# Running decay preparation, attention and gated MoE of three groups of tokens side by side, with squares on ACT, the cosine by Abs and the state's scale carried by v

## The chip, the cores and the metric

The kernel runs on one core of a Trainium2 chip. The metric is device time in microseconds (us). Every kernel here was run several times, always beside runs of the kernel before on the same chip. The record marks a run as slow when it is over 1.5% above the fastest run of the same kernel; comparisons use the fast runs alone. ACT is the engine of activation functions, DVE the vector engine, POOL the GpSimd engine, PE the matmul engine, SP the queue that issues most transfers (SPq in the views), PEld the weight loads of PE. PSUM tiles hold the results of this kernel's matmuls. MoE is the gated layer after the attention. A slab is 128 tokens by 384 features (8 heads of 48); there are 24 slabs.

## The reference, cut to what matters

```python
# attention: q, k, v, a_re, a_im of shape (4, 8, 768, 48)
mag = np.sqrt(a_re * a_re + a_im * a_im)
scale = np.minimum(mag, 0.999) / (mag + 1e-06)
a = (a_re + 1j * a_im) * scale            # written here as one complex number
for t in range(S):
    state = a[:, :, t, :, None] * state + k_t (outer) v_t
    y[:, :, t] = q_t @ real(state)
# MoE: x = y as (3072, 384); w_gate, w_val (384, 1536); w_out (1536, 384)
out = (sigmoid(x @ w_gate) * (x @ w_val)) @ w_out
```

The kernel turns the recurrence into matmuls inside slabs: the logarithms of the magnitudes are summed along the tokens by a matmul with a triangular matrix (`cl`), so are the angles (`ct`), and q and k are multiplied by the exponentials, sines and cosines of the sums.

## The kernel before

Eight groups of three slabs each. In the first half of a period PE has the attention of group g, the output projection of g-1 and the decays of g+1 (`prep_a`); in the second half gate and value of g and the angles of g+1 (`prep_b`). ACT's instructions stay in the order in which the program gives them.

Names in the code and in the views: `cl` and `ct` are the summed logarithms and angles (the matmul with `nid_t` takes whole turns `r` off the angles), `cs` their cosine and sine, `kst` and `qst` the products of k and q with them. In attention `tp` are the transposes of q and k (`qkT` their copy), `sc` the scores (`mst` masked), `kv`, `u`, `P` and `x` belong to the state, `xp` are the transposes of y. In the MoE `pg`, `pv` and `po` are the matmuls of gate, value and output, `g` is the tanh of the gate, `p` gate times value. `lm`, new in the changed kernel, is the squared magnitude and then its logarithm.

```python
    def prep_a(g):                                   # decays
        nc.scalar.preload_act_table_set("natural_log_exp_and_others")      # L157
        nc.scalar.activation(out=ar, in_=ar, func=FT.Ln)
        nc.scalar.activation(out=inv, in_=ar, func=FT.Exp, scale=-1.0)
        yield
        for s in range(NS):
            G.last_pool = nc.gpsimd.tensor_tensor(                         # L162
                out=ai[:, s], in0=ai[:, s], in1=inv[:, s], op=ALU.mult)
            nc.scalar.activation(out=inv[:, s], in_=ai[:, s], func=FT.Square)
            nc.scalar.activation(out=inv[:, s], in_=inv[:, s], func=FT.Ln, bias=1.0)
            nc.vector.scalar_tensor_tensor(                                # L167
                out=ar[:, s], in0=ar[:, s], scalar=2.0, op0=ALU.mult,
                in1=inv[:, s], op1=ALU.add)
            nc.vector.tensor_scalar(out=ar[:, s], in0=ar[:, s],            # L170
                                    scalar1=LN_CAP, scalar2=None, op0=ALU.min)
            yield
        # ... per slab: cl = wl_t @ ar (L176), two Exp of cl, products with q and k on POOL
    # prep_b, cosine of one slab:
            r2 = psm.tile([L, HD], F16, name=f"r2_{g}_{s}", tag="r2")
            nc.vector.tensor_scalar(out=r2, in0=ct, scalar1=0.25,          # L229
                                    scalar2=None, op0=ALU.is_gt)
            nc.tensor.matmul(ct, nid_t, r2, start=False, stop=True, ...)
            nc.scalar.activation(out=cs[:, 0], in_=ct, func=FT.Sin,
                                 scale=TWO_PI, bias=pio2)
    # attn, one slab: state (u, x16, kv), transposes, scores, y, transposes of y;
    # then the next slab.  main loop:
        for g in range(NG):
            st = [(attn(g), 21)]
            if g > 0:
                st.append((outproj(g - 1), 9))
            if g + 1 < NG:
                loads_a(g + 1); loads_q(g + 1)
                st.append((prep_a(g + 1), 7))
            merge(*st)
            st = [(gateval(g), 12)]
            if g + 1 < NG:
                st.append((prep_b(g + 1), 4))
            merge(*st)
```

## Time and profile before

| | before |
|---|---|
| time, median of 3 runs | 383.69 us |
| span of the profiled run | 382.3 us |
| ACT's log table loads for the decays of groups 1 to 7 | 46.29 to 302.22 us, so 42.7 us a period |
| from the last of these loads to the end | 80.1 us |
| granted PE clock, mean | 0.902 |

One more view is needed for what came later, the groups of instructions on PE. In a row, after the bar come busy time and mean ns of one, then the idle time of PE just before these instructions and who ended it.

```profile
L176 PE MATMUL cl<-a,wl_t 128*128 128x384 f32 x48 | 29.8, 724 | 14.3 <-DVE a L170 14.3
L296 PE MATMUL sc<-qkT 128*128 128x128 f16 x192 | 21.9, 245 | 22.1 <-DVE qkT L288 21.9
L319 PE MATMUL xp<-idn_t,y 128*128 128x128 f16 x72 | 9.5, 250 | 14.9 <-ACT y L314 14.6
```

PE stood 37 us in all in front of the scores (sc) and the transposes of y (xp), which depend on a result made moments before, and 14 us in front of the decay matmul cl. The 14 us all lie in the start, before 46.29 us.

### The profile page before, as it was taken

The page shows a single profiled execution, that of the slowest core. Times are in us where ns is not written, and L with a number is a line of the kernel's source. Part 1 is how long each engine was busy: PE and PEld are TensorE (multiplying, and loading weights), DVE is VectorE, ACT ScalarE, POOL GpSimd, SP SyncE. Part 2 cuts the span into 40 slices and gives each one's busy share as a digit, 9 for nine tenths or more (in the row PEclk, how much of TensorE's full clock was granted, in tenths as well). Part 3 has the DMA queues.
Part 4 walks back from the last instruction along what each step waited for, and adds up shares of the span by engine and source line. Part 5 has one row for each costly group of instructions (what it writes and reads, how often), then busy time and mean ns, then how long its engine had stood idle before and what let it go on. Part 6 is the DMA issues. An engine that isn't in the chain of part 4 may idle for free.

```text
span 382.3 us, 6035 instructions
## 1 busy us (share of the span) xinstructions
PE 291.6 (76%) x2208; PEld 179.5 (47%) x2208; DVE 244.3 (64%) x451; ACT 199.8 (52%) x343; POOL 107.1 (28%) x114
## 2 busy tenths in 40 slices
PE   0451448899579958898679958898679958998796
PEld 0121135456445636455445536465445645555463
DVE  1325476478735994678736895688727995589450
ACT  2650253846467554846376554747375645731241
POOL 0755444412353035302152035303132035200000
PEclk9988557999799987999699988999699988999899
DMA  9998993996654771465432772054410002000101
GB/s 155 191 204 127 197 172 63 141 176 119 127 97 77 119 144 43 63 100 87 103 70 37 105 144 44 1 107 83 103 22 3 0 22 42 2 0 22 43 2 62
DMA packets 150989, 32.68 MB, mean 85 GB/s; under 512 B 145048, under 2 KB 150192, under 8 KB 150960
## 3 DMA queue, kind: packets, MB, share of 16 engines
q1 hardware_dynamic: 148368, 28.76, 42.5%
q0 software_dynamic: 2592, 3.54, 5.2%
q8 instruction: 17, 0.28, 0.3%
q14 instruction: 12, 0.10, 0.1%
HBM read 31.07 MB, written 4.76 MB: 94 GB/s over the span
## 4 chain that ended last, share of the span: by engine, by line
issue 33%; PE 26%; DVE 12%; ACT 9%; POOL 7%; DMA 6%; SPq 5%; POOLq 0%; ACTq 0%
PE cl L176 6%; DMA qk<-in_k_dram 5%; DVE mst L300 4%; PE pg L330 4%; DVE a L167 3%; PE po L347 3%; PE pv L334 3%; POOL run L217 3%; SPq L109 3%; DVE qkT L288 2%; ACT y L314 2%; POOL a L162 2%; PE xp L319 2%; PE tp L285 2%; PE tp L284 2%
## 5 line engine op out<-in xcount | busy, mean ns | idle before, releaser
L330 PE MATMUL pg<-xt,wg 128*128 128x384 f16 x288 | 64.5, 329 | 7.5 <-ACT g L337 5.7
L191 POOL TENSOR_TENSOR qk<-qk,ee 128x768 f32<-128x768 f32 x24 | 43.9, 1829 | 74.4 <-ACT ee L179 45.2
L334 PE MATMUL pv<-xt,wv 128*128 128x384 f16 x288 | 63.2, 329 | 0.0
L338 DVE SCALAR_TENSOR_TENSOR p<-g,pv 128x384 f16<-128x384 f16 x96 | 49.4, 549 | 21.1 <-ACT g L337 17.6
L162 POOL TENSOR_TENSOR a<-a,inv 128x384 f32<-128x384 f32 x24 | 24.8, 1060 | 114.3 <-ACT inv L159 114.3
L337 ACT ACTIVATE g<-pg 128x384 f16<-128x384 f32 x96 | 43.9, 489 | 21.7 <-PE pg L330 21.6
L347 PE MATMUL po<-wo,p 128*128 128x384 f16 x288 | 54.7, 325 | 0.1
L330 PEld LDWEIGHTS <-wg 128*128 128x128 f16 x288 | 28.3, 98 | 35.3 <-issue 18.5
L288 DVE COPY qkT<-tp 128x1024 f16<-128x1024 f16 x48 | 32.3, 684 | 13.9 <-PE tp L285 13.7
L176 PE MATMUL cl<-a,wl_t 128*128 128x384 f32 x48 | 29.8, 724 | 14.3 <-DVE a L170 14.3
L296 PE MATMUL sc<-qkT 128*128 128x128 f16 x192 | 21.9, 245 | 22.1 <-DVE qkT L288 21.9
L334 PEld LDWEIGHTS <-wv 128*128 128x128 f16 x288 | 28.4, 99 | 19.9 <-issue 1.6
L221 DVE TENSOR_SCALAR r<-ct 128x384 f16<-128x384 f32 x24 | 13.3, 554 | 33.3 <-PE ct L210 17.8
L233 ACT ACTIVATE cs<-ct,pio 128x384 f32<-128x384 f32 x24 | 14.0, 581 | 38.9 <-PE ct L231 38.9
L300 DVE TENSOR_TENSOR mst<-sc,msk_t 128x512 f16<-128x512 f32 x48 | 31.4, 681 | 3.3 <-PE sc L296 3.2
L347 PEld LDWEIGHTS <-p 128*128 128x128 f16 x288 | 25.9, 97 | 14.6 <-issue 1.1
L284 PE MATMUL tp<-idn_t,qst 128*128 128x128 f16 x192 | 32.7, 250 | 0.0
L285 PE MATMUL tp<-idn_t,kst 128*128 128x128 f16 x192 | 32.3, 250 | 0.0
L177 ACT ACTIVATE ee<-cl 128x384 f32<-128x384 f32 x24 | 11.8, 492 | 37.4 <-PE cl L176 37.4
L237 DVE TENSOR_TENSOR qst<-qk,cs 128x768 f16<-128x768 f32 x24 | 23.0, 958 | 12.3 <-ACT cs L233 10.6
L296 PEld LDWEIGHTS <-qkT 128*128 128x128 f16 x192 | 14.1, 108 | 35.6 <-DVE qkT L288 31.4
L314 ACT ACTIVATE y<-y 128x384 f16<-128x384 f32 x24 | 11.7, 489 | 36.5 <-PE y L311 36.5
(57 smaller groups left out, 498.4 us busy)
## 6 DMA issues: line engine op xcount, KB each, us to landing
a<-in_a_re_dram SPq DMA_DIRECT2D x24, 192.0 KB
a<-in_a_im_dram SPq DMA_DIRECT2D x24, 192.0 KB
qk<-in_q_dram SPq DMA_DIRECT2D x24, 192.0 KB
qk<-in_k_dram SPq DMA_DIRECT2D x24, 192.0 KB
v<-in_v_dram SPq DMA_DIRECT2D x24, 192.0 KB
out_dram<-ot SPq DMA_DIRECT2D x24, 192.0 KB
wg<-in_moe_w_gate_dram POOLq DMA_DIRECT2D x3, 384.0 KB, 9.0
wv<-in_moe_w_val_dram POOLq DMA_DIRECT2D x3, 384.0 KB, 8.7
```

Of the source, the lines that this page charges most:

```text
L176: nc.tensor.matmul(cl, wl_t, ar[:, s], start=True, stop=True)
L191: nc.gpsimd.tensor_tensor(out=G.qk[:, :, s], in0=G.qk[:, :, s], in1=G.ee[:, :, s], op=ALU.mult)
L284: nc.tensor.transpose(tp[:, i], qs[:, h], idn_t)
L285: nc.tensor.transpose(tp[:, 4 + i], ks[:, h], idn_t)
L288: nc.vector.tensor_copy(out=qkT, in_=tp)
L296: nc.tensor.matmul(sc[:, i], qkT[:, 4 + i], qkT[:, i], start=True, stop=True)
L300: nc.vector.tensor_tensor(out=mst, in0=sc, in1=msk_t.unsqueeze(1).broadcast_to([L, 4, L]), op=ALU.mult)
L330: nc.tensor.matmul(pg, wg16[:, j, fc], G.xt[:, j], start=(j == 0), stop=(j == 2))
L334: nc.tensor.matmul(pv, wv16[:, j, fc], G.xt[:, j], start=(j == 0), stop=(j == 2))
L337: nc.scalar.activation(out=g16, in_=pg, func=FT.Tanh, scale=0.5)
L338: nc.vector.scalar_tensor_tensor(out=G.p[:, fb], in0=g16, scalar=1.0, op0=ALU.add, in1=pv, op1=ALU.mult)
L347: nc.tensor.matmul(po, G.p[:, fb, s * L:(s + 1) * L], wo16[:, fb], start=(fb == 0), stop=(fb == NFB - 1))
```

## The change

Its intent: (1) three stages at once, attention of group i, MoE of i-1 and i-2, preparation of i+1, so that large MoE matmuls stand beside every short dependent one; groups of uneven size (1, 2, 3 x 6, 2, 1), so that the pipeline fills and drains on small groups; (2) the decays from |a| squared: squares on ACT, add and clamp on POOL, one Ln for a group, which frees DVE; (3) the cosine as sin(pi/2 - |x|), with Abs on ACT in place of a comparison on DVE and a second matmul; (4) the scale 1024 of the state carried by v, so that DVE does not multiply it in; (5) inside attention, the transposes of slab s stand ahead of the end of slab s-1. Cut to its core (buffers, tile shapes and names left out):

```diff
-    NS = 3
+    SIZES = [1, 2, 3, 3, 3, 3, 3, 3, 2, 1]
     def prep_a(g):
-        (Ln, Exp; per slab: POOL product, ACT Square, ACT Ln, DVE add, DVE min)
+        nc.scalar.activation(out=sq[:, :, :n], in_=G.a2[:, :, :n], func=FT.Square)   # L162
+        for s in range(n):
+            nc.gpsimd.tensor_tensor(out=G.lm[:, s], in0=sq[:, 0, s],                 # L165
+                                    in1=sq[:, 1, s], op=ALU.add)
+            nc.gpsimd.tensor_scalar(out=G.lm[:, s], in0=G.lm[:, s], scalar1=CAP,     # L167
+                                    scalar2=-1.0, op0=ALU.min, op1=ALU.max)
+        nc.scalar.activation(out=ar, in_=ar, func=FT.Ln)
+        nc.scalar.activation(out=ar, in_=ar, func=FT.Exp, scale=-1.0)
+        yield
+        nc.scalar.activation(out=lm, in_=lm, func=FT.Ln)                             # L173
     # prep_b
-            nc.vector.tensor_scalar(out=r2, in0=ct, scalar1=0.25, op0=ALU.is_gt, ...)
-            nc.tensor.matmul(ct, nid_t, r2, ...)
+            nc.scalar.activation(out=cs[:, 0], in_=ct, func=FT.Abs)
     # attn
-                nc.vector.tensor_scalar(out=x16, in0=u, scalar1=YSC, op0=ALU.mult)
+                nc.gpsimd.tensor_copy(out=X[s], in_=u)
-        for each slab: state, turn 0, turn 1, score 0, score 1, yout, xput
+        for s in range(n + 1):
+            turn(s, 0); turn(s, 1); state(s)       # if s < n
+            xput(s - 1)                            # if s > 0
+            score(s, 0); score(s, 1); yout(s)      # if s < n
     # main loop, iteration i
+            merge(first 2/5 of attn(i), outproj(i - 2), prep_a(i + 1))
+            merge(rest of attn(i), gateval(i - 1), prep_b(i + 1))
```

## The prediction

> **What bounds the kernel now.** I read the page first (busy shares, then the 40 slices), then the windows of one period, its timeline on PE and ACT, and the waits.
>
> ```profile
> span 382.3 us, 6035 instructions
> PE 291.6 (76%) x2208; PEld 179.5 (47%) x2208; DVE 244.3 (64%) x451; ACT 199.8 (52%) x343; POOL 107.1 (28%) x114
> PE   0451448899579958898679958898679958998796
> PEclk9988557999799987999699988999699988999899
> DMA  9998993996654771465432772054410002000101
> ```
> No engine is full, and PE breathes: four or five slices at 8 or 9, then one or two at 5 to 7 with the clock at 6 or 7. DMA is full only in the first 17 slices. The table load ahead of the first tanh on ACT marks a period for three slabs of 128 tokens: in the timeline it starts at 110.83, 152.57, 196.19, 238.09, 281.62 and 323.30 us, so **41.7 to 43.6 us**, mean 42.5, each. Windows of the two halves of one period (gate/value with the angles of the next group, then attention with the decays of the next):
>
> ```profile
> core 0: us, PE busy (x) PEld busy (x) DVE busy (x) ACT busy (x) POOL busy (x), PEclk, DMA share, GB/s
> 260.55:281.62 21.07, 15.24 (x151) 10.05 (x149) 14.12 (x26) 11.66 (x21) 6.62 (x5) 0.84 0.42 85
> 238.09:260.55 22.46, 20.95 (x131) 12.28 (x129) 16.90 (x29) 13.35 (x22) 4.30 (x4) 1.00 0.32 54
> ```
> The second row is bound by PE (21 of 22.5 us, full clock). The first is bound by nothing: PE is open for 6 us and slow for part of the rest. It is a chain of latencies:
>
> ```profile
> 264.29 3.01 POOL L162 TENSOR_TENSOR a<-a,inv 128x384 f32<-128x384 f32 x3 [18.49 <-ACT inv L159]
> ...
> 268.37 0.40 PE L296 MATMUL sc<-qkT 128*128 128x128 f16 x4 [2.28 <-DVE qkT L288]
> 269.71 0.40 PE L296 MATMUL sc<-qkT 128*128 128x128 f16 x4 [0.94 <-DVE qkT L288]
> ...
> 272.51 1.59 PE L176 MATMUL cl<-a,wl_t 128*128 128x384 f32 x2
> ```
> Prep goes ACT, POOL, ACT, DVE before PE gets its decay matmul, and attention goes PE, DVE, PE, DVE, ACT, PE; both queue for DVE, and the large MoE matmuls that could fill PE are in the other half.
>
> **Real PE work in a period**, from spacings of starts in the timeline at full clock: 36 po start 0.163 us apart, transposes 0.055, the 48-column matmuls 0.025, one f32 matmul takes 0.65. So pg, pv, po 108 x 0.163 = 17.6; tp, sc, xp 81 x 0.055 = 4.5; kv, y 64 x 0.025 = 1.6; cl, ct, on 8.5 x 0.65 = 5.5; nid 6 x 0.163 = 1.0. Sum **30.2 us** of 42.5, 71%. Eight groups: 242 us.
>
> **What the Trainium skill says.** (1) "TensorE: Matmul & The Clock Gate", Part 1: after an idle window of about 3.4 us the PE clock halves until the array has been busy for another. The trace agrees: clock 0.84 in the first row, and transposes 0.107 us apart near 274 us against 0.055. Filling PE's gaps thus pays twice. (2) Same page, "Step-by-step" of a matmul: only weight loads are pulled ahead; matmuls stay in program order. So a matmul whose input is late holds up ready MoE matmuls behind it; PE's waits on qkT above agree. (3) "GPSIMD Engine Reference", Engine selection: two-input elementwise is about twice as slow as VectorE, one-input about line rate. The rows agree: 1060 ns on POOL for a product of 384 columns, against some 550 on DVE; the cast takes 551. (4) "ScalarE: Activation LUTs", table sets: abs and copy are in every set, a load is 1283 ns. The load is 1283 in the trace; for Abs no run shows it yet, but the built order has no load in front of it.
>
> **The change, engine by engine.**
>
> ```profile
> L167 DVE SCALAR_TENSOR_TENSOR a<-a,inv 128x384 f32<-128x384 f32 x24 | 18.6, 773 | 13.3 <-ACT inv L165 13.3
> L170 DVE TENSOR_SCALAR a<-a 128x384 f32<-128x384 f32 x24 | 8.5, 354 | 0.1
> L229 DVE TENSOR_SCALAR r<-ct 128x384 f16<-128x384 f32 x24 | 13.3, 554 | 4.2 <-ACT cs L226 3.7
> L264 DVE TENSOR_SCALAR x<-u 128x384 f16<-128x384 f32 x20 | 12.1, 605 | 0.4
> L164 ACT ACTIVATE inv<-a 128x384 f32<-128x384 f32 x24 | 12.3, 514 | 5.8 <-POOL a L162 5.8
> L165 ACT ACTIVATE inv<-inv 128x384 f32<-128x384 f32 x24 | 12.6, 523 | 0.8
> ```
> DVE loses the first four: 52.5 us, so 244 to about **195** (24 more, shorter p products add a little). PE loses one nid matmul per slab, 3.9 us: **238** of real work. POOL gains 24 adds (1.06), 24 clamps and 20 state copies and 4 angle copies (0.55 each, taken from the cast): 25 + 13 + 13, so 107 to **159**. ACT loses 24.9; it gains squares (0.845 ns a column from the 384- and 1152-column rows: 17), one Ln per group (10), 24 Abs (12), 7 more table loads (38 in the built order against 31: 9), and fixed costs of ten groups instead of eight with 120 tanh (5): 200 to **228**. All four fit beside each other in about 240 us. What counts is how well they overlap, and ACT's program order is fixed.
>
> **One iteration of three full groups**, walked through the built order. t = 0 is ACT's first table load. Load 1.28 and Square of 2304 columns 2.17: 3.45. POOL then does three adds, three clamps and one state copy, 5.0 (ACT's Ln, Exp and an output copy fit beside it): 8.5 to 8.9. Ln 1.16: 10.1, and only now the decay matmul cl. In front of cl PE has po 5.9, transposes 0.9, kv and sc 0.4, one pg/pv pair 1.0: 8.2, begun 1.6 before zero. So PE stands for about **3 us**. Six Exp, two output copies and one y at 0.4, with the waits for cl and y between: 15.8. Then load, tanh, load, Arctan, load: 21.3. PE has 5.8 us of work since cl; gate/value cannot run on, as four PSUM tiles hold two pairs, and then it stands for ct until the Arctan ends at 20.0: again about **3 us**. From 20.0 PE has ct and on 3.6, nine pairs 8.8, nid 0.5, transposes, scores and y 2.9: 15.8, so 35.8; Abs and two Sin 1.5: 37.5. DVE has some 18 us of work in the same 16 (11 p at 0.5, six q/k products at 0.95, masks, copies), which I count as 0.5 more. Period **38**, against 42.5.
>
> **The ends.** Ramp: the first attention is of one slab and starts near 18 us instead of 30. But the squares of the third group wait for all of a of its slabs. By then the constants 0.4, five inputs of three slabs 2.9, one q of the next group 0.2, its a 1.2 and the weights 3.5 MB have to land (0.197 MB a load of a slab; as 3.54 MB in queue 0): 8.2 MB, and the GB/s row of before had moved 8.35 MB by 47.8 us (packets stay under 512 B). So the second iteration starts at about **46**, as in the kernel before, when three slabs are prepared in both. Then: iteration 1 (prep of three slabs, MoE of one) 29; 2 and 3 with less MoE 33 and 37; three full ones 114; iteration 7 (prep of two) 33; iteration 8 26; 9 16; 10 8.5; 11 with the last output 5. Sum 46 + 301.5 = 347.5 of span, and some 1.4 more in the time (383.7 against 382.3). The tail pays: before took 37.3 us after 345.0, its last group alone on PE; here three iterations take 29.5 and carry two groups' outputs.
>
> **Rivals.** (A) PE stays fed: the two holes of 3 us are filled, as weight loads and transposes are spread finely, and the clock stays full. Then the period is 33 to 34 us (30 of PE work plus one hole): 4.5 x 6 = 27 less, 320. For it: PE was at 93% in the half where MoE lay beside prep. (B) ACT becomes the bound: 28 us of work a period in fixed order, seven waits on other engines in it, and each late input holds tanh, hence PSUM tiles, hence PE. With a microsecond more at each stage end, and a half clock after each 3 us hole, the period is 40 to 41: 365. Against it: much of ACT's work is back to back at 0.39 us. (C) The start stays bound by DMA with smaller groups, and POOL's longer list (three adds, clamps, products) delays q and k: iterations 1 and 2 grow by 10: 357. (D) Nothing is gained, period 42.5: the sum becomes about 375, still 2% less by the shorter tail. I see no way to slower but POOL blocking DVE[...]: DVE's L167 took up to 1312 ns beside POOL and 546 without.
>
> **Range.** I take 345: my sum less a little for A. A and C/B bound it: 324 to 366 for 8 in 10. Same needs the period of before with no gain in the tail.
>
> **What would show it.** Right: table loads of steady iterations 38 us apart; DVE near 195, ACT near 228, POOL near 159 us; PE idle before cl behind lm on ACT and POOL, and before ct behind Arctan, about 3 us each; PEclk at 9 in most slices after 46 us; third group's Square ending a DMA wait near 46 us. Wrong: clamps on POOL far from 0.55 us; PE waiting for DVE (qkT, p) rather than for ACT; the ramp ending well before or after 46; a period under 34 or over 41.

## More of the kernel before

The timeline shows the decay chain of one group from its table load to the last Ln on ACT, then, on DVE, the clamp that ends the decays of its first slab (start, duration, engine, line, operation):

```profile
260.55 1.28 ACT L157 ACT_TABLE_LOAD   x1
...
268.28 0.52 ACT L165 ACTIVATE inv<-inv 128x384 f32<-128x384 f32 x1
...
268.24 0.34 DVE L170 TENSOR_SCALAR a<-a 128x384 f32<-128x384 f32 x1
```

## The result, and the profile after

The changed kernel took **373.12 us** (median of 4 runs, 372.34 to 375.02) against 383.6 (382.49 to 384.45): faster, with a ratio of 0.9736 (95% interval 0.9691 to 0.9781), but outside the predicted range of 324 to 366. A ratio is the mean time of one kernel's fast runs over that of the other's fast runs of the same rounds, so it is not quite the ratio of the medians quoted. The page of after, first lines of its busy times and slices:

```profile
span 371.3 us, 6375 instructions
...
PE 277.8 (75%) x2328; PEld 181.4 (49%) x2328; DVE 206.1 (55%) x385; ACT 224.0 (60%) x376; POOL 157.7 (42%) x186
...
PE   0310753595569937997889967996799899999996
PEclk9999995899589968899889989998999999999999
```

The totals of DVE, ACT and POOL came out within 6% of what was worked out, but PE's load rises and falls as before: the digits drop to 5, 6 and 7 between groups. The log table loads on ACT (L161) divide the run into iterations. They start at 51.17, 86.61, 126.06, 167.09, 207.24, 246.38, 285.37 and 318.87 us. Four of the iterations as windows (columns: window in us, its length, then busy us and count on PE, PE weight loads, DVE, ACT, POOL, then clock, DMA share and GB/s):

```profile
51.17:86.61 35.44, 21.56 (x215) 15.38 (x216) 19.68 (x42) 21.96 (x38) 19.99 (x22) 0.81 0.90 138
86.61:126.06 39.45, 27.95 (x249) 20.15 (x246) 24.80 (x44) 24.00 (x41) 20.07 (x24) 0.83 0.56 96
...
207.24:246.38 39.14, 33.16 (x275) 21.15 (x274) 24.75 (x45) 26.27 (x42) 17.97 (x19) 0.96 0.47 87
...
285.37:318.87 33.50, 31.06 (x285) 19.92 (x283) 25.86 (x44) 22.66 (x38) 12.85 (x13) 1.00 0.14 31
```

The iteration that starts at 86.61 has MoE work of smaller groups than the one at 207.24, and 5 us less on PE, yet it is no shorter. The first row, with MoE of one slab and attention of two, has 11.6 us less on PE and is 3.7 shorter; the last, with full MoE but two slabs to prepare, is 5.6 shorter. So the length follows the preparation more than the MoE work. Where PE stands, in the groups of after:

```profile
L182 PE MATMUL cl<-lm,wl_t 128*128 128x384 f32 x48 | 30.5, 737 | 60.3 <-ACT lm L173 60.3
L304 PE MATMUL sc<-qkT 128*128 128x128 f16 x192 | 21.0, 241 | 0.5 <-DVE qkT L296 0.2
L331 PE MATMUL xp<-idn_t,y 128*128 128x128 f16 x72 | 8.3, 219 | 0.3 <-ACT y L324 0.3
```

The waits for sc and xp are gone, from 37 us to under 1. One other wait has grown from 14.3 to 60.3 us: the decay matmul behind the Ln on ACT. By the timeline of PE, 24.8 us of it lie before iteration 1, where the kernel before had its 14.3, and 35.5 in iterations 1 to 8, where the kernel before had none. The timeline of one iteration, on ACT, POOL and PE, shows what that Ln waits for:

```profile
207.24 1.28 ACT L161 ACT_TABLE_LOAD   x1
208.53 2.12 ACT L162 ACTIVATE sq<-a 128x2304 f32<-128x2304 f32 x1
...
210.74 2.29 POOL L165 TENSOR_TENSOR lm<-sq 128x384 f32<-128x384 f32 x2 [3.91 <-ACT sq L162]
213.11 1.09 POOL L167 TENSOR_SCALAR lm<-lm 128x384 f32<-128x384 f32 x2
...
216.34 1.16 ACT L173 ACTIVATE lm<-lm 128x1152 f32<-128x1152 f32 x1 [2.91 <-POOL lm L167]
...
217.56 0.91 PE L182 MATMUL cl<-lm,wl_t 128*128 128x384 f32 x2 [3.45 <-ACT lm L173]
```

From the table load to cl it is 10.3 us (207.24 to 217.56); the matmul needs the end of POOL's list first, 5.7 us after the Square's end at 210.65. In the kernel before, the decays came slab by slab: those of the first slab were ready 8.0 us after the load (268.24 + 0.34 - 260.55), the last Ln ended after 8.3, and the third slab's clamp, behind other work on DVE, after 11.8. PE, busy with attention, began cl at 272.51 without waiting for it.

The start was late too: the iteration meant to begin at 46 us began at 51.17. ACT stood 11.6 us for the second group's input (first line); the third group's Square waited for nothing (second line).

```profile
30.73 1.48 ACT L162 ACTIVATE sq<-a 128x1536 f32<-128x1536 f32 x1 [11.60 <-DMA a<-in_a_im_dram]
...
52.46 2.12 ACT L162 ACTIVATE sq<-a 128x2304 f32<-128x2304 f32 x1
```

### The profile page after: what moved, and what is told of

Its sections match the earlier page's. It is cut to its first block, busy times and chain, and to the rows that moved or that the text cites. A ratio compares the mean times of both kernels' runs of the same rounds, so it can differ in the third digit from the quotient of the medians.

```text
span 371.3 us, 6375 instructions
## 1 busy us (share of the span) xinstructions
PE 277.8 (75%) x2328; PEld 181.4 (49%) x2328; DVE 206.1 (55%) x385; ACT 224.0 (60%) x376; POOL 157.7 (42%) x186
## 4 chain that ended last, share of the span: by engine, by line
PE 42%; ACT 21%; POOL 11%; DVE 9%; DMA 8%; issue 5%; SPq 3%; ACTq 0%; DVEq 0%; POOLq 0%
PE pg L362 8%; PE cl L182 8%; PE pv L367 7%; POOL lm L165 5%; PE ct L215 4%; PE po L381 3%; ACT sq L162 3%; POOL lm L167 3%; ACT lm L173 3%; DMA wv<-in_moe_w_val_dram 3%; DVE qst L242 2%; PE sc L304 2%; PE ct L218 2%; ACT L161 2%; ACT L208 2%
## 5 line engine op out<-in xcount | busy, mean ns | idle before, releaser
L182 PE MATMUL cl<-lm,wl_t 128*128 128x384 f32 x48 | 30.5, 737 | 60.3 <-ACT lm L173 60.3
L370 ACT ACTIVATE g<-pg 128x384 f16<-128x384 f32 (+2 forms) x120 | 49.5, 427 | 41.8 <-PE pg L362 35.5
L362 PE MATMUL pg<-xt,wg 128*128 128x384 f16 (+2 forms) x360 | 67.6, 296 | 7.6 <-ACT g L370 7.3
L367 PE MATMUL pv<-xt,wv 128*128 128x384 f16 (+2 forms) x360 | 68.8, 295 | 1.9 <-DVE p L371 1.1
L371 DVE SCALAR_TENSOR_TENSOR p<-g,pv 128x384 f16<-128x384 f16 (+2 forms) x120 | 54.8, 468 | 23.8 <-ACT g L370 19.5
L165 POOL TENSOR_TENSOR lm<-sq 128x384 f32<-128x384 f32 x24 | 25.8, 1089 | 41.1 <-ACT sq L162 40.6
L362 PEld LDWEIGHTS <-wg 128*128 128x128 f16 x360 | 31.8, 99 | 22.2 <-issue 12.2
L182 PEld LDWEIGHTS cl<-lm,wl_t 128*128 128x128 f32 x48 | 10.5, 265 | 64.4 <-ACT lm L173 63.2
L215 PE MATMUL ct<-a,wt_t 128*128 128x384 f32 x48 | 25.0, 607 | 12.8 <-ACT a L209 12.8
L242 DVE TENSOR_TENSOR kst<-qk,cs 128x768 f16<-128x768 f32 x24 | 23.1, 960 | 7.9 <-ACT cs L238 5.4
L162 ACT ACTIVATE sq<-a 128x2304 f32<-128x2304 f32 (+2 forms) x10 | 17.4, 1740 | 14.7 <-DMA a<-in_a_im_dram 14.6
L292 PEld LDWEIGHTS <-kst 128*128 128x128 f16 x192 | 20.3, 107 | 8.1 <-DVE kst L242 4.8
```

Of the source, the lines that this page charges most:

```text
L165: nc.gpsimd.tensor_tensor(out=G.lm[:, s], in0=sq[:, 0, s], in1=sq[:, 1, s], op=ALU.add)
L182: nc.tensor.matmul(cl, wl_t, G.lm[:, s], start=True, stop=True)
L215: nc.tensor.matmul(ct, wt_t, th[:, s], start=True, stop=False, skip_group_check=True)
L292: nc.tensor.transpose(tp[:, 4 + i], G.ks[s][:, h], idn_t)
L362: nc.tensor.matmul(pg, wg16[:, j, fc], G.xt[:, j, :nt], start=(j == 0), stop=(j == 2))
L367: nc.tensor.matmul(pv, wv16[:, j, fc], G.xt[:, j, :nt], start=(j == 0), stop=(j == 2))
```

## The experiments

Sixteen kernels were run, each timed in 3 rounds (4 runs each). Beside them the kernel before had medians of 383.2 to 383.9. The first theory was: an iteration is a chain (ACT, POOL, ACT, PE, ACT, then the angles) of nearly fixed length, and the new decay arithmetic made it longer. The rival: PE's work, or DVE's, sets the length.

**1. Weights issued later** (`e1_weights_late`), for the ramp.

```diff
-        with tc.issue_after(gs[0].last_pool.ins):
-            load_weights()
+            if i == 0:   # gate and value weights after group 1's POOL work, output weights later
```

> Only the loads of the MoE weights move: gate and value after the prep of the second group, out after its angles. Theory A (the weights, issued from 8.65 us, hold back a of the second group, for which ACT waited 11.6 us until 30.7): that wait falls under 3 us, the second iteration starts (third load of the log table on ACT) near 41 us instead of 51.2, and the time is about 363 us instead of 373. Rival (the bytes of the first 46 us bound the ramp in any order, as the prediction had it): the wait only moves to a of the third group or to the weights themselves, second iteration at 47 or later, time 369 or more.

Measured 367.05 us, ratio 0.9592. Iteration 1 began at 40.13 in place of 51.17, as the theory had it, and ACT no longer waited for the second group's input; but the iteration took 40.8 in place of 35.4. POOL was still issuing output weights at 47 us and delayed the next decays' add. So of 11 us of start 6 were kept: the weights' loads stand in it, and about half of what moving them gains returned as another wait.

**2. Add and clamp on DVE** (`e7_lm_dve`), two instructions a group in place of two a slab on POOL.

```diff
-        for s in range(n):
-            nc.gpsimd.tensor_tensor(out=G.lm[:, s], in0=sq[:, 0, s], in1=sq[:, 1, s], op=ALU.add)
-            nc.gpsimd.tensor_scalar(out=G.lm[:, s], in0=G.lm[:, s], scalar1=CAP, ...)
+        nc.vector.tensor_tensor(out=lm, in0=sq[:, 0, :n], in1=sq[:, 1, :n], op=ALU.add)
+        nc.vector.tensor_scalar(out=lm, in0=lm, scalar1=CAP, scalar2=-1.0, ...)
```

> Add and clamp of the squares move from POOL (six instructions of 0.5 to 1.1 us a group) to two DVE instructions over the whole group, about 2.1 us, which fit beside Ln and Exp on ACT. Theory B (an iteration is a chain from squares to decays to angles, whatever MoE work lies beside it): the wait of the second Ln behind POOL, 2.9 to 3.5 us an iteration, goes, PE's wait for the decay matmul shrinks by the same, full iterations go from 39.4 to about 36.5 us, time about 352. Rival (PE and ACT are busy enough that the second half takes up the slack, or POOL's other work then ends the wait): full iterations at 38 or more and a time of 365 or more.

Measured **347.09 us**, ratio 0.9064 (0.902 to 0.9108): 26 us from the add and the clamp moved. Its timeline (ACT, then DVE):

```profile
191.23 1.28 ACT L161 ACT_TABLE_LOAD   x1
...
197.36 1.16 ACT L171 ACTIVATE lm<-lm 128x1152 f32<-128x1152 f32 x1
...
194.71 1.35 DVE L164 TENSOR_TENSOR lm<-sq 128x1152 f32<-128x1152 f32 x1
...
196.58 0.75 DVE L166 TENSOR_SCALAR lm<-lm 128x1152 f32<-128x1152 f32 x1
```

The Ln starts 6.1 us after the table load (197.36 - 191.23) where it was 9.1 (216.34 - 207.24). The three full iterations fell from 40.2, 39.1 and 39.0 to 34.7, 34.7 and 35.6, all of it in the first part (16.6 to 12.1), while the second stayed at 22.6. Beyond the Ln's 3.0 us there is a gain behind cl: PE's transposes, 0.11 us apart after the long wait in the changed kernel (220.40 to 221.57), are 0.055 apart here. Over the whole kernel the wait for cl fell from 60.3 to 39.8 us. DVE did more work and the kernel was faster: DVE's total was not the limit.

**3. A third of the gate and value matmuls** (`e3_third_gate`), and the same with the short chain (`e15_lm_dve_third_gate`). Their outputs are wrong, which doesn't matter for the times.

```diff
-            for j in range(3):
-                nc.tensor.matmul(pg, wg16[:, j, fc], G.xt[:, j, :nt], start=(j == 0), stop=(j == 2))
+            nc.tensor.matmul(pg, wg16[:, 0, fc], G.xt[:, 0, :nt], start=True, stop=True)
```

> Wrong result on purpose: gate and value contract over one of three blocks, so a full iteration has 48 matmuls of 384 columns less, 7.8 us of PE work (62 us in all). Theory B: the first part of an iteration (from the log table load to the tanh table load) stays at 16.5 us, with a longer hole of PE ahead of the decay matmul; the second part, 22.6 us, gives back about half of what leaves it, so full iterations are about 35 us and the time about 345. Rival (PE's sum of work sets the iteration, as the prediction had it for its second part and for the iterations with less MoE): 31.5 us an iteration, time 315 or less.

> Wrong result on purpose: three stages with the add and clamp on DVE (347), with one of the three matmuls of each gate and value tile, so some 62 us of PE work less. Theory, a chain through ACT, POOL, DVE and PE sets the iteration, MoE work or not: 347 - 12 = 335, full iterations 33 to 35. Rival, with the short chain PE sets it: full iterations lose the 7.8 us of matmuls each, 27 to 29, and the time is 290 to 305.

Measured 361.27 (ratio 0.9441), 12 less than the changed kernel, and 337.24 (0.8774), 10 less than experiment 2, for about 62 us of PE work removed (an estimate: 384 matmuls of 384 columns at the prediction's 0.163 us). The same iteration with all matmuls, then with a third of them:

```profile
191.23:225.96 34.73, 31.71 (x276) 19.96 (x274) 28.16 (x47) 26.12 (x43) 13.50 (x13) 1.00 0.56 97
```

```profile
187.59:222.69 35.10, 27.24 (x228) 16.29 (x227) 26.47 (x48) 25.85 (x42) 13.17 (x13) 0.95 0.53 95
```

This iteration is not shorter, and no engine is full in it; the three full ones of the short chain took 35.7, 35.1 and 33.8 us against 34.7, 34.7 and 35.6, a mean 0.2 less. This is the clearest run: **the full iterations are not bound by PE**. (The granted clock fell too, from 1.00 to 0.95 here, so that some of the cut came back as slower matmuls; but PE is idle for 8 of the 35 us.) Where PE does count is the end: of the 13.0 us by which the profiled run is shorter, 7.9 were gained from the start of iteration 7 on, and 9.9 of 12.3 without the short chain. What runs in the second part, in the timeline of DVE of this run:

```profile
206.38 0.56 DVE L227 TENSOR_SCALAR r<-ct 128x384 f16<-128x384 f32 x1 [3.86 <-PE ct L216]
...
211.47 0.96 DVE L240 TENSOR_TENSOR kst<-qk,cs 128x768 f16<-128x768 f32 x1 [0.48 <-ACT cs L236]
...
216.11 0.96 DVE L240 TENSOR_TENSOR kst<-qk,cs 128x768 f16<-128x768 f32 x1 [0.23 <-ACT cs L236]
...
222.78 0.95 DVE L240 TENSOR_TENSOR kst<-qk,cs 128x768 f16<-128x768 f32 x1
```

DVE waits 3.9 us for the first angles, behind two table loads and the Arctan on ACT. From then to the third slab's kst at 222.78 it is nearly back to back: the angles' r, the products with sines and cosines, and the gates' p stand in one queue in program order, and a slab's next step stands behind the gates' p. That this queue sets the length is read from the timeline, not tested.

**4. The old decays in the new schedule** (`e2_old_decays`): the kernel before's `prep_a` arithmetic put back, all else as changed.

```diff
-        (Square; POOL add and clamp; Ln, Exp; Ln of lm; products)
+        (Ln, Exp; per slab: POOL product, ACT Square, ACT Ln, DVE add, DVE min)
```

> The new schedule with the old arithmetic of the decays: ratio on POOL, Square and Ln of it on ACT, sum and cap on DVE, slab by slab. DVE gains about 27 us of work, POOL loses 38, ACT about 2. Theory B: the first decay matmul waits for a chain of about 8.5 us from the log table load instead of 10.3, later ones follow by slabs; an iteration is 1.5 to 2 us shorter and the time about 360. Rival (unloading DVE is what the change gains): slower than the change, 380 or more.

Measured **350.25 us**, ratio 0.9149 (0.9105 to 0.9192). Undoing part (2) of the change gains 23 us, 10 more than expected.

**5. Even groups** (`e4_even`), and **two stages with even groups** (`e5_two_stage`), both with all of the new arithmetic and attention order.

```diff
-    SIZES = [1, 2, 3, 3, 3, 3, 3, 3, 2, 1]
+    SIZES = [3] * 8
```

```diff
-            merge(first part of attn(i), outproj(i - 2), prep_a(i + 1))
-            merge(rest of attn(i), gateval(i - 1), prep_b(i + 1))
+            merge(attn(g), outproj(g - 1), prep_a(g + 1))
+            merge(gateval(g), prep_b(g + 1))
```

> Eight groups of three slabs in place of ten uneven ones, all else as in the change. Theory B (an iteration costs its chain, 39 us with three slabs in prep and 35 even with little MoE beside it): the first prep is longer, and two iterations fall away, which about cancel: 370 to 380 us. Rival (the small first and last groups are what fills ramp and tail, as intended): 385 or more, no faster than the kernel before.

> The schedule and the even groups of the kernel before, with all the new arithmetic (squares on ACT, add and clamp on POOL, cosine by Abs, state and v scaled on POOL) and the new order within attention. Theory B: the longer chain to the decays (10.3 us to the first matmul against 8) is in the first half of each period there too, though DVE is freer in it: a period of 42 to 44 us and 375 to 395 us in all, so the arithmetic gains nothing alone. Rival (the arithmetic is what gained, the schedule nothing): 373 or less.

Measured 372.18 (0.9694) and 368.32 (0.9594). Between uneven and even groups no difference is clear of the noise (the intervals of the ratios overlap), and the old schedule is 5 us faster than the new one. That was the rival's number. The first run also shows an iteration with no MoE work at all beside the preparation of three slabs: 35.0 us (46.44 to 81.39), with no wait of ACT for a transfer, against 39 to 41 for those with MoE work. So about nine tenths of an iteration stay without it.

**6. The two schedules with a short decay chain** (`e12_two_stage_old_decays`, `e13_two_stage_lm_dve`): is the new schedule worth something once its chain is short? The edits are those of 4 and 2 on top of 5.

> The kernel before's schedule (two stages, even groups) and its decay arithmetic, with only the change's other arithmetic and attention order (Abs cosine, state scaled through v, split turns and scores). With the new decays the same schedule took 368; the three-stage schedule took 373 with the new decays and 350 with the old. Theory S, the three-stage schedule is worth something once the decay chain is short: about 362 here, so some 12 more than the three-stage kernel with the same decays. Rival R, the schedule is worth nothing and only the arithmetic counts: 345 to 352, as three stages with the same decays.

> The kernel before's schedule with the change's whole arithmetic, but the add and the clamp of the squares done on DVE as two instructions a group, as in the three-stage run that took 347. In the two-stage run with the change's own decays PE waited 34.5 us for cl behind lm on ACT, 4.3 a group. Theory S: the wait shrinks by 3 to 4 us a group for the first half alone, but the rest of the half is attention and output work that fills PE: about 360, 13 more than three stages. Rival R: all of the wait is gained, 368 - 8 x 2.6 = 347, and the schedule is worth nothing.

Measured 343.89 (0.8966, 0.892 to 0.9012) and 340.77 (0.8871, 0.8823 to 0.892): my theory fell, and both came out below even the rival's numbers. The schedule against the decays, medians in us:

| | new decays (POOL) | old decays | add and clamp on DVE |
|---|---|---|---|
| two stages, even | 368.3 | 343.9 | 340.8 |
| three stages, uneven | 373.1 | 350.3 | 347.1 |

In every column three stages are slower, by 5 to 6 us (the intervals of the ratios do not overlap), and in each row the new decays cost 23 to 28. The last column's traces give the account: with two stages the second group's table load comes at 46.6 us, six periods of 37.0 follow, and 71.0 remain; with three stages it is 48.8, seven iterations of 35.0, and 52.0. So a period is shortened by only 2, the tail by 19, and one more iteration has to be paid: 2.2 + 22.7 - 19.0 = 5.9 more.

**7. Two stages with a third of the gate and value matmuls** (`e16_two_stage_lm_dve_third_gate`, wrong result).

> Wrong result on purpose: the same cut in the two-stage run that took 341. Theory: in two stages the half with gate and value is as much a chain (angles for the next group) and the other half is untouched by the cut: 341 - 15 = 326. Rival, PE-bound in the gate and value half: it loses up to 7.8 us a group, 341 - 62 = 280 to 300.

Measured 338.89 (0.8832), only 2 less than with all matmuls (340.77), which is within the noise. In one such half PE's busy time fell from 18.2 to 14.4 us, and the half stayed at 19.8 and 19.9. (The mean granted clock of the profiled runs fell from 0.955 to 0.914, so some of the cut came back here too.) The half with gate and value is not bound by PE here either, less so than I had expected. This accounts for three stages gaining so little: they make room for PE work, and PE work is not what the full periods of either schedule wait for.

**8. The old cosine** (`e8_old_cos`): the comparison on DVE and the second nid matmul back in the changed kernel.

```diff
-            nc.scalar.activation(out=cs[:, 0], in_=ct, func=FT.Abs)
+            nc.vector.tensor_scalar(out=r2, in0=ct, scalar1=0.25, op0=ALU.is_gt, ...)
+            nc.tensor.matmul(ct, nid_t, r2, start=False, stop=True, ...)
```

> The changed kernel with one part undone: the cosine by a comparison on DVE and a second nid matmul in place of Abs on ACT. Theory: the second part of an iteration is bound by DVE's in-order queue together with PE, so 24 comparisons of 0.55 us (13 us of DVE), 24 matmuls on PE and the detour ACT, DVE, PE, ACT cost nearly their DVE time: 373 + 10 = 383. Rival: the iteration is a chain through ACT, and taking 24 Abs of 0.5 us off ACT pays for the comparison: 370 to 376.

Measured 387.4 (1.0104): Abs is worth 14 us, about the 13 of DVE time that it removes. The run also puts back a matmul and a round trip over DVE and PE for each slab and takes an Abs off ACT, so what of the 14 is DVE's time alone is not shown.

**9. The old order of attention** (`e14_old_order`), on the run of 343.89.

```diff
-        (turn, turn, state of slab s; xput of slab s - 1; score, score, yout of slab s)
+        (state, turn, turn, score, score, yout, xput of slab s, one slab after another)
```

> The run with the kernel before's schedule and decays that took 344, with the order of the attention's steps put back too (a slab's transposes, scores, output and output transposes one after the other, state first); what is left of the change is Abs in the cosine, k before q, the state's scaling and the split of gate and value. In the kernel before PE waited 21.9 us for qkT on DVE and 14.6 for y on ACT, in the run of 344 2.1 and under 9. Theory: the new order gains most of the 26 us that the Abs leaves unexplained: 344 + 20 = 364. Rival: the gain is DVE work taken away (the state's scaling, 12 us) and the order is neutral: 344 to 350.

Measured 362.63 (0.945, 0.9381 to 0.9518), so the order is worth 19 us, as the theory had it. Its PE groups show about half of the kernel before's wait for sc back again, and all of that for xp:

```profile
L301 PE MATMUL sc<-qkT 128*128 128x128 f16 x192 | 20.2, 232 | 10.5 <-DVE qkT L293 9.8
...
L328 PE MATMUL xp<-idn_t,y 128*128 128x128 f16 x72 | 8.8, 236 | 15.3 <-ACT y L321 15.3
```

In the run of 343.89 these were 2.5 and 7.4. The new order has a wait of its own: there y stood 14.5 us for the state's copy on POOL, and in this run it did not.

**10. The q product on POOL** (`e10_q_pool`), to relieve DVE in the second part.

```diff
-                nc.vector.tensor_tensor(out=dst..., in0=G.qk[...], in1=cs..., op=ALU.mult)
+                (nc.vector if i == 0 else nc.gpsimd).tensor_tensor(out=dst..., ...)
```

> The product of q with the cosines and sines moves from DVE to POOL, which stands for some 14 us in the second part; three products of 0.95 us leave DVE in each iteration. Theory C (in the second part DVE's queue, not PE, is the bound: with a third of the gate matmuls its length did not change): the second part goes from 22.6 to about 20.5 us, time about 358. Rival (PE bounds the second part, or POOL with its slower products of two inputs holds q back): second part 22.5 or more, time 371 or more.

Measured 388.78 (1.0079); one of the four runs was slow, and the fast ones have a median of 387.55: 14 us slower than the changed kernel, against an expected gain. The DVE and POOL groups of this run:

```profile
L242 DVE TENSOR_TENSOR kst<-qk,cs 128x768 f16<-128x768 f32 x24 | 56.7, 2362 | 8.2 <-ACT cs L238 6.8 <-issue 1.3
...
L242 POOL TENSOR_TENSOR qst<-qk,cs 128x768 f16<-128x768 f32 x24 | 45.2, 1885 | 71.5 <-ACT cs L238 71.5
```

The k product that stayed on DVE rose from 960 ns in the changed kernel to 2362, while POOL did the q product beside it. DVE spent 56.7 us on one product where it had spent 46.2 on both. In the timeline the two start together, at 244.11 and 244.10 us, and take 2.61 and 1.81. "GPSIMD Engine Reference", 1. Specifications, in the Trainium skill says that POOL shares its SBUF interfaces with the vector engine and contends with DVE instructions of two SBUF inputs; the runs agree.

**11. Arctan first** (`e6_arctan_first`): the angles' first step ahead of the gates in the second part, so the tanh table is loaded once less.

```diff
-                st.append((prep_b(i + 1), 1 + 2 * sz(i + 1)))
+                pb = prep_b(i + 1)
+                next(pb)
+                st.append((pb, 2 * sz(i + 1)))
```

> Arctan, with its table loads, is put ahead of the first tanh, y copy and gate of the second part, so one table load and one or two copies (1.8 us) leave ACT's chain from the last Exp to Arctan. Theory B: the wait of ct for Arctan comes 1.8 us earlier in each of eight iterations, full iterations 37.5 us, time about 360. Rival (the second part is bound by DVE or PE work of its own, which starts no earlier for it): 369 or more.

Measured 367.1 (0.9574), between theory and rival: a gain of 6, whose split between the earlier start and the load saved I cannot tell.

**12. Versions meant to beat both.** `c1_three_mended` joins 1, 2 and 11 in three stages; `c5_two_stage_mended` joins 2 and 11 in two stages and even groups.

> A version meant to beat both: the changed kernel with the add and clamp on DVE, the weights' loads issued later, and the Arctan issued before the second part's other ACT work. One by one these gave 347, 367 and 367 against 373, so gains of 26, 6 and 6. Theory, they lie in different places (first part, ramp, second part) and add: 373 - 38 = 335 to 340. Rival, each shortens the same chain or only moves POOL's weight issues under the next iteration: 344 to 348, no better than the first alone.

> A version meant to beat both: two stages and even groups, the change's arithmetic with the add and clamp on DVE (341), and the Arctan issued before the gate and value half's other ACT work. It gained 6 in three stages, and with the weights' loads 12 on top of 347. PE waited 12.0 us for ct behind Arctan in the run of 341. Theory: the tanh table is then loaded once less a group and the angles start 2 us sooner: 341 - 8 = 333. Rival: gate and value's first tanh is now late, PE stands for its PSUM tiles instead: 339 to 344.

Measured 335.48 (0.8735) and **331.21 us** (0.8627, 0.8582 to 0.8673), both correct. In three stages the gains added (38 expected and measured); in two stages the Arctan gained 9.6, where 8 was expected. The best version has the old schedule with the new arithmetic.

## Why the prediction was right or wrong

The direction was right; the time was 28 us too low. In its own steps:

**The engine totals** were nearly right: DVE 195 predicted, 206 measured; ACT 228 and 224; POOL 159 and 158. So were **the clamp** at 0.55 us on POOL (1.09 for two) and the add at 1.06 (1.09 on average).

**One full iteration** was nearly right: 38 predicted, 40.2, 39.1 and 39.0 measured, with its first part 15.8 against 16.6, and the hole in front of cl 3 against 3.5 (its own numbers, 10.1 less 6.6, give 3.5). The hole in front of ct was 1.2, not 3. Reading a chain off the built order of ACT worked for the first part. The reading of the second part, that PE's 15.8 us of work set it, did not: experiment 3 took a quarter of PE's real work away and the iteration stayed. (Two slips of the text change nothing: 20.0 + 15.8 + 1.5 is 37.3, not 37.5; and the DMA row is near full in the first nine slices, not seventeen.)

**The step that failed** is the ends: "iteration 1 (prep of three slabs, MoE of one) 29; 2 and 3 with less MoE 33 and 37". I priced these by their PE work, and tied the start to the bytes of the third group. Measured:

| term of the sum | predicted | measured | difference |
|---|---|---|---|
| start of iteration 1 | 46 | 51.2 | +5.2 |
| iteration 1 | 29 | 35.4 | +6.4 |
| iteration 2 | 33 | 39.5 | +6.5 |
| iteration 3 | 37 | 41.0 | +4.0 |
| iterations 4 to 6 | 114 | 118.3 | +4.3 |
| iteration 7 | 33 | 33.5 | +0.5 |
| the rest | 55.5 | 52.4 | -3.1 |
| span | 347.5 | 371.3 | +23.8 |

The rest of the 28 us is that I took 345 where my sum gave 348.9, and that the median is 1.8 above the span where I added 1.4. With less MoE work the chain in an iteration does not shrink; PE's wait for cl grows instead. From the table load to cl it is 10.3 to 10.5 us in each of iterations 1 to 6, and 7.1 in iteration 7 with two slabs; the wait was 8.7, 8.0 and 6.3 us in iterations 1 to 3 and 3.5 in 4 to 6. I had this chain on the page already, since the walk through a full iteration set its times by ACT and POOL up to 21.3 us, whatever the MoE does; I did not apply it to the small ones.

**The start** failed in its path, not only by 5 us. The prediction let iteration 1 wait until 8.2 MB had landed, the third group's a last. The bytes were right: at 181 GB/s (the window 0 to 46 us) 8.3 MB had moved by 46. But the third group's Square did not wait. What set the start was the second group's a, for which ACT stood until 30.73, and the 20.4 us of iteration 0 behind it. Experiment 1 shows it: with the weights' loads moved that wait was gone and iteration 1 began at 40.1, before the bytes would have let it by the prediction.

**DVE's 18 us in the second part, counted as 0.5**: the total came out nearly right there (22.6 measured against 22.2), but by luck, as the reason that I gave does not hold. I took 15.8 us of PE as the bound and DVE as hidden. In experiment 3 a third of the matmuls leaves the part as long, while in experiment 8 one short DVE instruction a slab more, with its matmul and round trip, costs about as much as its DVE time. The same goes for the reading of the kernel before's gate and value half as bound by PE (21 of 22.5 us): experiment 7 took PE work out of that half in the two-stage schedule and it stayed as long; in the kernel before itself this was not run.

**The clock.** The trace shows the half clock (0.50 from 274 to 277 us in the kernel before), but not the idle window of 3.4 us that the prediction names for it: from 265 to 277 us PE's longest pause was 2.3 us.

**The rivals.** (A) fell: PE is not kept fed, and the period was 39 to 40, not 33. (B) ACT's order as the bound was nearest in kind, the holes being behind ACT and POOL. (C) explains part: the start was 5 late and iterations 1 and 2 together were 13 longer, where C had 10, though by the decays' wait. (D) came nearest in size, 375, and its first words, "Nothing is gained", are what the experiments show of the schedule, but the period did fall and the tail's gain was eaten by the extra iteration. The POOL and DVE contention showed in the change too, not only where I added to it (experiment 10): the state's product u on DVE, with the same shape, rose from 578 to 874 ns on average, 6 us in all; the longest, 2.05 us at 105.22, lay beside a POOL product of 1.80 at 105.06. How much of this reached the time was not tested.

**What I did not ask** is which part of the change gains. The chain of runs answers: before 383.7; Abs, the state's scale, k before q, the split of gate and value and more buffers together -21 (experiment 9's run, 362.6), of which Abs would be 14 by experiment 8, measured in the other schedule; the new order of attention -19 (343.9); the new decays +24 (368.3); the three-stage schedule over uneven groups +5 (373.1). The expected gain went into the chain of the decays: the order of attention removed waits of 37 us, and the wait for cl in the iterations rose from none to 35.5 us. The parts of the -21 other than Abs were not run one by one, so their shares stay open. The steps of this chain come from different rounds, so each is good to 1 to 3 us only. What limits the second part exactly, DVE's queue order or the round trips between ACT, PE and DVE inside it, was not separated either; only that PE's amount of work is not it.

## What to carry to other kernels

Before giving a pipeline more stages, find out whether its iteration is bound by work or by a chain, by cutting most of the work of the suspected engine in a kernel that may be wrong: if the iteration stays as long, more room for that engine buys little, and every extra iteration costs the whole chain again. When work is moved to a free engine, look whether it stands in the chain that starts each iteration; here moving a cheap add and clamp from the idle engine to the busier one gained 26 us of the whole. Price an iteration with less work by the longest chain in it, not by its share of the work. Before a start is put down to the bytes that it needs, look which instruction waits for which transfer, and what was issued ahead of it.

## What the Trainium skill lacked or had wrong

- "ScalarE: Activation LUTs", What ACT_TABLE_LOAD costs, gives 1283 ns for a load and about 1380 ns of drain more. The load is 1283 ns in the trace; no drain of that size shows: the instruction before the load at 207.24 us ended at 207.23 (206.59 + 0.64), and the next one started at 208.53.
